# Two of batch 1's head pairs: x transposed by a DMA through the crossbar in place of TensorE, in a fused attention and GELU MLP kernel

## The chip, the cores and the metric

One core of one Trainium2 chip. The metric is the device time of one execution in microseconds. Engines: PE (TensorE; PEld its weight loads), DVE (VectorE), ACT (ScalarE), POOL (GpSimd) and SP (SyncE, which here only issues DMAs), and 16 DMA engines that carry the transfers of all queues.

## What is computed

The inputs are q, k, v of 8 batches x 8 heads x 576 tokens x 64, forget gates f of 8 x 8 x 576, and the weights w_in (512 x 2048) and w_out (2048 x 512), all float32.

```python
scores = (1 / sqrt(64)) * q @ k.T                     # per batch and head
cum    = cumsum(log(clip(f, 1e-4, 1)), axis=-1)
scores = where(causal, -1e9, scores + cum[:, None] - cum[None, :])
attn   = softmax(scores)                              # over the keys
x      = (attn @ v), heads side by side               # 4608 x 512
h      = x @ w_in
out    = (0.5 * h * (1 + erf(h / sqrt(2)))) @ w_out   # 4608 x 512
```

## The kernel before

Batches run one after the other. In each, the eight heads are taken as four pairs, since two heads of 64 fill 128 partitions.

**Attention of a pair.** `scores(b, i, t)` multiplies kT by qT into a tile of the score pool (two buffers of PSUM), four tiles t per pair; ACT takes the exponential (L313) and POOL zeroes the half above the diagonal (L315), except in batch 0 and pair 0 of batch 1, where PE adds the mask. `attend` multiplies the exponentials by the weighted v (L334); the decay is folded into v as a factor per key, which POOL multiplies in (`weigh_v`, L272). `normalize` divides by the row sums on DVE and writes x of the pair (L347, L348): 128 tokens x 5 blocks x 128 (two heads x 64), bfloat16.

**x to xT.** The MLP's first product needs x with the model dimension on the partitions. There are two ways in the program. `to_xT(b, i, ...)` has PE transpose five 128x128 blocks into a PSUM buffer (L367), and DVE or ACT copies that into `xT` (L370). `x_dma(b, i)` issues one DMA_TRANSPOSE from SBUF to SBUF on SP's queue (L373), straight into `xT`. Batches 0 and 1 use `to_xT` for all four pairs; batches 2 to 7 use `x_dma` for all four.

**MLP.** `gemm1` multiplies w_in by xT in 16 blocks of the hidden dimension, of four matmuls each (L389), and ACT takes the GELU (L409). The second product is interleaved with the next batch's attention (`gemm2_first` L529, `gemm2_second` L553, `gemm2_rows` L493, `take(fill, n)` issuing n of its steps). A batch has 576 = 512 + 64 tokens; the 64 left over are kept in `tails` (`x_tail`, POOL, L379) and multiplied last, for all batches together (L389 and L433 at the end).

**The order around the change.** The program fixes the order by hand; every engine takes its instructions in the order in which the program issues them, and an instruction waits for the semaphores of what it reads and of the buffer that it writes. In `second_attention` (batch 1) PE's order is: score tiles and attention of pairs 0 to 3, with `gemm1_hold` (six blocks of batch 0's GEMM1, kept in SBUF for a later GELU) and `gemm2_first` in between; then `gemm1_begin`, whose first matmuls read pairs 0 and 1 of xT, and the rest of batch 1's GEMM1. `gemm2_third` follows in batch 2's attention, beginning with `gemm2_second`: its first 8 steps write two banks of the PSUM pool "o", which DVE adds to `ot` (L561, then L513 through `sum_out`), its next 8 two banks of pool "m" in the same way; then `gemm2_rows` takes the two "o" banks again (L493).

**Transfers.** POOL's queue (q0) loads with a cast from float32 to bfloat16: q and k of the next batch (`load_qk_tokens`, L109), w_in and w_out (L171, L175), and v of batch 1 (L121). SP's queue (q1) carries v of later batches (L121), the transposes, and the stores (L517). From batch 2 on, q and k are transposed by DMA as well: `transpose_dma(2, 0, 4)` and `(2, 4, 8)` issue a tq and a tk transpose for four heads each (L239), on SP; tq waits for q, tk for k. DVE's `untangle` then puts them into qT and kT (L253), for pairs 0 to 3 of batch 2 at hidden blocks 5, 8, 11 and 14 of batch 1's GEMM1, ahead of the additions L561 and L513 in DVE's order. `behind(qk_of[2][1], H - 1)` is a POOL copy that reads the last of batch 2's k (L579), so that the last two w_out loads are issued after k has landed.

Of the kernel before, what the change touches and what calls it, by code (L numbers as in the profile page):

```python
# [53 lines left out]
def kernel(  # L54
# [10 lines left out]
    nc = tc.nc  # L65
# [25 lines left out]
    o_psum = ctx.enter_context(tc.tile_pool(name="o_psum", bufs=2, space=PSUM))  # L91
# [81 lines left out]
    def load_w_out(c):  # L173
        kt = slice(c * n_ff // 4, (c + 1) * n_ff // 4)
        nc.gpsimd.dma_start(w_out_sb[:, kt, :], w_out_r[:, kt, :])  # L175
# [27 lines left out]
    def transposes_first(b, i, which, pool, tag, late=False):  # L203

        src = qk_of[b][which]
        ps = pool.tile([P, JT, PT], BF16, tag=tag, name="ps_f")
        for j in range(JT):
            for h in range(2):
                nc.tensor.transpose(  # L209
                    ps[h * D : (h + 1) * D, j, :],  # L210
                    src[:, 2 * i + h, j * D : (j + 1) * D],
                    ident_bf[:PT, :PT],
                )

        dst = (qT, kT)[which][i].rearrange("d (p j) -> d p j", j=JT)
        src = ps.rearrange("d j p -> d p j")
        if late:
            return partial(nc.vector.tensor_copy, dst, src)
        if b or i:
            nc.vector.tensor_copy(dst, src)  # L220
        elif which:
            nc.vector.tensor_copy(dst[:, 0 : PT // 2], src[:, 0 : PT // 2])
            nc.scalar.copy(dst[:, PT // 2 :], src[:, PT // 2 :])
        else:
            nc.scalar.copy(dst, src)
# [3 lines left out]
    def transpose_dma(b, h0, h1):  # L229

        if b >= B:
            return
        if b not in tq_of:
            tq_of[b] = [
                tq_pool.tile([P, H, JT // 2, PT], BF16, tag="t" + n, name=f"t{n}{b}")
                for n in "qk"
            ]
        for src, dst in zip(qk_of[b], tq_of[b]):
            nc.sync.dma_start_transpose(  # L239
                dst[:, h0:h1].rearrange("d h j p -> d (h j) p"),  # L240
                src[:, h0:h1].rearrange("p h c -> p (h c)"),
            )
# [19 lines left out]
    def vw(b):  # L262
        if b not in vw_of:
            vw_of[b] = v_pool.tile([P, H, NBLK, D + 1], BF16, tag="vw", name=f"vw{b}")
        return vw_of[b]

    def weigh_v(b, i, eng=nc.gpsimd, n0=0, n1=NBLK):

        hs = slice(2 * i, 2 * i + 2)
        bh = b * H + 2 * i  # L270
        w = wT[:, n0:n1, bh : bh + 2].rearrange("p n h -> p h n")
        eng.tensor_tensor(  # L272
            vw(b)[:, hs, n0:n1, 0:D],
            v_sb[:, hs, n0:n1, :],
            w.unsqueeze(3).to_broadcast([P, 2, n1 - n0, D]),
            Alu.mult,
        )
        if b:
            eng.tensor_copy(vw(b)[:, hs, :, D], w)
# [47 lines left out]
    def attend(b, i, h, ms, pool=o_psum, tag="o"):  # L327
        if (b, i, h) not in o_of:
            o_of[b, i, h] = pool.tile([P, NBLK, D + 1], FP32, tag=tag, name="o")
        o = o_of[b, i, h]  # L330
        for m in ms:
            for n in range(m + 1):
                t, c = where(n, m)
                nc.tensor.matmul(  # L334
                    o[:, m, :],
                    e_of[b, i, t][:, h, c : c + P],
                    vw_of[b][:, 2 * i + h, n, :],
                    start=(n == 0),
                    stop=(n == m),
                )  # L340

    def normalize(b, i, h):
        if (b, i) not in x_of:
            x_of[b, i] = x_pool.tile([P, NBLK, 2, D], BF16, tag="x", name="x")
        o = o_of[b, i, h]
        r = x_pool.tile([P, NBLK], FP32, tag="r", name="r")
        nc.vector.reciprocal(r, o[:, :, D])  # L347
        nc.vector.tensor_tensor(  # L348
            x_of[b, i][:, :, h, :],
            o[:, :, 0:D],  # L350
            r.unsqueeze(2).to_broadcast([P, NBLK, D]),
            Alu.mult,
        )

    def xT(b):
        if b not in xT_of:
            xT_of[b] = xT_pool.tile([P, n_dm, XC], BF16, tag="xT", name="xT")
        return xT_of[b]

    def to_xT(b, i, copy, pool=m_psum, tag="m", ps=None):  # L360
        if ps is None:
            shape = [P, 2, 1024] if pool is s_psum else [P, XC]
            ps = pool.tile(shape, BF16, tag=tag, name="ps_x")
            if pool is s_psum:
                ps = ps[:, 0, 0:XC]
        for m in range(NBLK):
            nc.tensor.transpose(  # L367
                ps[:, m * P : (m + 1) * P], x_of[b, i][:, m, :, :], ident_bf
            )
        copy(xT(b)[:, i, :], ps)  # L370

    def x_dma(b, i):
        nc.sync.dma_start_transpose(  # L373
            xT(b)[:, i, :].rearrange("d (m p) -> d m p", p=P),
            x_of[b, i].rearrange("p m h d -> p (m h d)"),
        )
# [37 lines left out]
    def gemm1_hold(ffb, copy=nc.vector.tensor_copy):  # L414
        ps = gemm1(0, ffb, act=False)
        h_of[ffb] = h_pool.tile([P, TC], FP32, tag=f"h{ffb}", name=f"h{ffb}")
        copy(h_of[ffb], ps)
# [103 lines left out]
    def gemm2_first(c):  # L521

        pss = [
            m_psum.tile([P, d_model], FP32, tag="m", name="ps2") for _ in range(2)
        ]
        for kq in (0, 4):
            for ts in range(2):
                for kt in range(kq, kq + 4):
                    nc.tensor.matmul(  # L529
                        pss[ts],  # L530
                        g_of[c][kt][:, ts * P : (ts + 1) * P],
                        w_out_sb[:, kt, :],
                        start=(kt == 0),
                        stop=(kt == 7),
                    )
                    if kt == 7:
                        ot_of.append(
                            o_pool.tile([P, d_model], FP32, tag="ot", name="ot")
                        )
                        copy = nc.scalar.copy if ts else nc.vector.tensor_copy  # L540
                        copy(ot_of[ts], pss[ts])
                    yield
# [27 lines left out]
    def take(gen, n):  # L570
        for _ in range(n):
            if next(gen, "end") == "end":
                return


    def behind(t, h):

        g = x_pool.tile([P, 1], FP32, tag="gate", name="gate")
        nc.gpsimd.tensor_copy(g[:PT], t[:, h, 0:1])  # L579
# [166 lines left out]
    def second_attention():  # L746


        b, fill = 1, gemm2_first(0)

        def av(i, h):
            attend(b, i, h, (0, 1, 2, 3, 4))
            normalize(b, i, h)

        def transposes(i, pool, tag):
            for which in range(2):
                transposes_first(b, i, which, pool, tag)


        nc.scalar.activation(warm[0:1, 0:1], warm[0:1, 0:1], Act.Exp)  # L760
        def tiles(i, t):
            scores(b, i, t)
            scores(b, i, t + 1)

        def run(i):
            av(i, 0)
            av(i, 1)

        tiles(0, 0)
        transposes(1, o_psum, "o")  # L770
        gemm1_hold(10)
        gemm1_hold(11)
        tiles(0, 2)
        gemm1_hold(12, nc.scalar.copy)
        transposes(2, o_psum, "o")
        tiles(1, 0)
        gemm1_hold(13)
        run(0)
        tiles(1, 2)
        gemm1_hold(14, nc.scalar.copy)  # L780
        transposes(3, o_psum, "o")
        weigh_v(1, 2)
        tiles(2, 0)
        gemm1_hold(15)
        run(1)
        weigh_v(1, 3)
        tiles(2, 2)
        take(fill, 4)
        tiles(3, 0)
        transpose_dma(2, 0, 4)  # L790
        transpose_dma(2, 4, 8)
        to_xT(b, 0, nc.vector.tensor_copy, o_psum, "o")
        to_xT(b, 1, nc.vector.tensor_copy, o_psum, "o")
        take(fill, 4)
        tiles(3, 2)
        behind(qk_of[2][1], H - 1)
        load_w_out(2)
        load_w_out(3)
        run(2)
        take(fill, 4)  # L800
        av(3, 0)
        take(fill, 4)
        both = s_psum.tile([P, 2, 1024], BF16, tag="s", name="ps_x2")
        to_xT(b, 2, nc.scalar.copy, ps=both[:, 0, 0:XC])
        av(3, 1)
        gemm1_begin(1, both)
        x_tail(1)
        load_v(2)
# [71 lines left out]
```

## Time and profile before

| | |
|---|---|
| three runs | 334.89, 335.05, 335.53 us (median 335.05) |
| the profiled execution | 337.87 us, its span 335.9 us |
| busy: PE | 325.7 us (97%) |
| busy: ACT | 206.6 us (61%) |
| busy: DVE | 184.2 us (55%) |
| busy: POOL | 133.0 us (40%) |
| granted TensorE clock | 1.0 throughout |
| DMA | 44.16 MB, mean 131 GB/s |
| xT<-x, issued by SP | 24 transposes, median 2.7 us from issue to landing |
| tq<-q, tk<-k, issued by SP | 12 and 12 transposes, median 4.2 and 4.3 us |

"Busy" is the time in which an engine executes something; the span is the profiled stretch from the first to the last instruction. In lines of the profile, L367 is line 367 of the kernel, `xT<-x` means that xT is written from x, and a bracket gives the idle time before an instruction and what ended it. Times in views are microseconds from the start of the span. The DMA share of a stretch can exceed 100% where an engine has more than one packet under way.

### The profile page before, as it was taken

How to read it: one execution, taken by the hardware profiler on the slowest of the kernel's cores; microseconds unless marked ns; L12 is line 12 of the kernel's file. 1: busy time of each engine (PE TensorE's matmuls, PEld its weight loads, DVE VectorE, ACT ScalarE, POOL GpSimd, SP SyncE). 2: the span in 40 equal slices, each digit the busy share in tenths (PEclk: the TensorE clock that was granted, in tenths of full speed). 3: DMA queues.
4: the chain of work that ended last, by engine and by line, in shares of the span. 5: the costliest groups of instructions: out<-in, count | busy, mean ns of one | idle time of the engine just before them, and what ended most of it. 6: DMA issues, size and time to landing. Idle time of an engine off the chain costs nothing.

```text
span 335.9 us, 7819 instructions
## 1 busy us (share of the span) xinstructions
PE 325.7 (97%) x3161; PEld 170.7 (51%) x3161; DVE 184.2 (55%) x424; ACT 206.6 (61%) x298; POOL 133.0 (40%) x260
## 2 busy tenths in 40 slices
PE   7779999999999999999999999999999999999995
PEld 3564555445554456445644555446544654444443
DVE  5671666594358945894579547964696550020011
ACT  4957886983734787378827882788378846404600
POOL 8787874029437044723445344525441420000000
PEclk9999999999999999999999999999999999999999
DMA  8999998999998799599947995769800231011012
GB/s 117 188 187 219 194 189 116 158 181 158 207 205 175 120 204 185 102 140 149 212 128 108 170 195 157 112 119 192 195 13 2 87 72 49 0 72 54 0 45 81
DMA packets 97427, 44.16 MB, mean 131 GB/s; under 512 B 75728, under 2 KB 92368, under 8 KB 97392
## 3 DMA queue, kind: packets, MB, share of 16 engines
q1 hardware_dynamic: 79344, 27.55, 41.6%
q0 software_dynamic: 17648, 15.60, 30.5%
q8 instruction: 24, 0.39, 0.5%
q10 hardware_dynamic: 400, 0.52, 0.4%
q14 instruction: 11, 0.09, 0.1%
HBM read 36.85 MB, written 9.44 MB: 138 GB/s over the span
## 4 chain that ended last, share of the span: by engine, by line
PE 90%; DMA 4%; POOL 2%; issue 1%; DVE 1%; ACT 0%; POOLq 0%; ACTq 0%
PE ps L389 36%; PE ps L493 26%; PE o L334 9%; PE ps L433 8%; PE s L303 7%; DMA v_sb<-in_v_dram 2%; DMA xT<-x 1%; PE ps L553 1%; PE ps_x L367 1%; PE ps L529 1%; PE ps_f L209 1%; POOL k L109 1%; POOL q L109 1%; DVE vw L272 0%; ACT e L313 0%
## 5 line engine op out<-in xcount | busy, mean ns | idle before, releaser
L409 ACT ACTIVATE g<-ps 128x512 bf16<-128x512 f32 x138 | 78.5, 601 | 79.8 <-PE ps L389 79.3
L313 ACT ACTIVATE e<-s 128x896 bf16<-128x896 f32 (+2 forms) x128 | 100.2, 835 | 23.8 <-PE s L303 18.7
L389 PE MATMUL ps<-xT,w_in_sb 128*128 128x512 bf16 x512 | 113.6, 379 | 0.1
L493 PE MATMUL ps<-w_out_sb,g 64*128 64x512 bf16 (+1 forms) x711 | 108.0, 377 | 0.0
L389 PEld LDWEIGHTS <-w_in_sb 128*128 128x128 bf16 x576 | 55.5, 98 | 67.4 <-issue 3.1
L315 POOL TENSOR_SCALAR_AFFINE_SELECT e<-e 128x256 bf16<-128x256 bf16 (+1 forms) x135 | 49.1, 383 | 90.1 <-ACT e L313 89.9
L493 PEld LDWEIGHTS <-g 64*128 64x128 bf16 (+1 forms) x711 | 39.4, 95 | 34.7 <-issue 4.2
L272 POOL TENSOR_TENSOR vw<-v_sb,wT 128x640 bf16<-128x640 f32 x30 | 38.7, 1290 | 26.1 <-DMA v_sb<-in_v_dram 15.3
L303 PE MATMUL s<-qT,kT 64*128 64x320 bf16 (+4 forms) x384 | 42.9, 276 | 1.5 <-ACT e L313 0.7
L253 DVE COPY kT<-tk 64x288 bf16<-64x288 bf16 x96 | 42.8, 446 | 1.6
L253 DVE COPY qT<-tq 64x288 bf16<-64x288 bf16 x96 | 40.0, 417 | 5.1 <-DMA tq<-q 3.7
L334 PEld LDWEIGHTS <-e 128*128 128x128 bf16 x960 | 34.7, 98 | 9.6 <-POOL e L315 2.9
L501 DVE COPY ot<-ps 128x512 f32<-128x512 f32 x20 | 13.8, 692 | 46.5 <-PE ps L493 46.5
L334 PE MATMUL o<-vw,e 128*128 128x65 bf16 x960 | 37.1, 194 | 1.3 <-DVE vw L272 1.3
L348 DVE TENSOR_TENSOR x<-o,r 128x320 bf16<-128x320 f32 x64 | 31.5, 492 | 3.1 <-DVE r L347 0.7
L442 DVE COPY ot<-ps 128x512 f32<-128x512 f32 (+2 forms) x9 | 5.7, 632 | 49.6 <-PE ps L433 49.6
L303 PEld LDWEIGHTS <-kT 64*128 64x128 bf16 x384 | 19.2, 94 | 21.5 <-issue 4.8
L433 PE MATMUL ps<-w_out_sb,g 128*128 128x512 bf16 (+2 forms) x144 | 28.0, 355 | 0.0
L433 PEld LDWEIGHTS <-g 128*128 128x128 bf16 x144 | 13.5, 98 | 14.5
L347 DVE RECIPROCAL r<-o 128x5 f32<-128x5 f32 x64 | 12.1, 188 | 11.3 <-PE o L334 11.3
L513 DVE TENSOR_TENSOR ot<-ot,ps 128x512 f32<-128x512 f32 x22 | 15.1, 685 | 1.1
L389 PE MATMUL ps<-tails,w_in_sb 128*128 128x512 bf16 x64 | 14.3, 378 | 0.0
(69 smaller groups left out, 153.6 us busy)
## 6 DMA issues: line engine op xcount, KB each, us to landing
out_dram<-ot SPq DMA_DIRECT2D x32, 256.0 KB, 2.4
v_sb<-in_v_dram SPq DMA_DIRECT2D x24, 256.0 KB, 4.8
q<-in_q_dram POOLq DMA_DIRECT2D x6, 576.0 KB, 6.3
k<-in_k_dram POOLq DMA_DIRECT2D x6, 576.0 KB, 8.4
w_in_sb<-in_moe_w_in_dram POOLq DMA_DIRECT2D x4, 512.0 KB, 8.0
w_out_sb<-in_moe_w_out_dram POOLq DMA_DIRECT2D x4, 512.0 KB, 9.2
v_sb<-in_v_dram POOLq DMA_DIRECT2D x13, 128.0 KB, 7.1
v_sb<-in_v_dram SPq DMA_DIRECT2D x9, 128.0 KB, 4.7
```

The lines of the kernel that those rows point to most:

```text
L253: nc.vector.tensor_copy(rows[:, odd], src[odd * D : (odd + 1) * D, 2 * i + h].rearrange("d j p -> d p j"),)
L272: eng.tensor_tensor(vw(b)[:, hs, n0:n1, 0:D], v_sb[:, hs, n0:n1, :], w.unsqueeze(3).to_broadcast([P, 2, n1 - n0, D]), Alu.mult,)
L303: nc.tensor.matmul(to, *ab, start=half < 0, stop=half == 1 or not masked)
L313: nc.scalar.activation(et[:, :, z:c], st[:, :, z:c], Act.Exp, scale=scale)
L315: nc.gpsimd.affine_select(out=et[:, :, c0 + z : c0 + P], in_=et[:, :, c0 + z : c0 + P], compare_op=Alu.is_ge, fill=0.0, base=z, pattern=[[ ...
L334: nc.tensor.matmul(o[:, m, :], e_of[b, i, t][:, h, c : c + P], vw_of[b][:, 2 * i + h, n, :], start=(n == 0), stop=(n == m),)
L348: nc.vector.tensor_tensor(x_of[b, i][:, :, h, :], o[:, :, 0:D], r.unsqueeze(2).to_broadcast([P, NBLK, D]), Alu.mult,)
L389: nc.tensor.matmul(ps, w_in_sb[:, kt, ffb * P : (ffb + 1) * P], src[:, kt, 0:TC], start=(kt == 0), stop=(kt == n_dm - 1),)
L409: nc.scalar.activation(g_of[c][ffb], ps, Act.Gelu)
L433: nc.tensor.matmul(pss[ts][:, c0:c1], g_of[c][kt][:, ts * P : (ts + 1) * P], w_out_sb[:, kt, c0:c1], start=(kt == 0), stop=(kt == n_ff - 1),)
L493: nc.tensor.matmul(banks[r], g_of[c][kt][rows, ts * P : (ts + 1) * P], w_out_sb[rows, kt, :], start=kt == (steps.index("r") if r else 0), ...
L513: nc.vector.tensor_tensor(ot, ot, bank, Alu.add)
```

## The change

In `second_attention`, batch 1's x of pairs 0 and 1 is no longer transposed by PE (`to_xT`, ten matmuls at L367 into two buffers of the pool "o", two DVE copies at L370). Instead `x_dma` is issued for each of the two pairs, right after the attention of that pair: pair 0 after `run(0)`, pair 1 after `run(1)`. On SP's queue both stand ahead of batch 2's transposes of q and k and of batch 2's v loads; before, nothing stood there between the first v loads of batch 0 and those transposes. Pairs 2 and 3 stay with PE. The first matmuls of batch 1's GEMM1 wait for the two transfers instead of the copies.

```diff
@@ second_attention
         gemm1_hold(13)
         run(0)
+        x_dma(b, 0)
         tiles(1, 2)
         gemm1_hold(14, nc.scalar.copy)
         transposes(3, o_psum, "o")
...
         gemm1_hold(15)
         run(1)
+        x_dma(b, 1)
         weigh_v(1, 3)
         tiles(2, 2)
         take(fill, 4)
         tiles(3, 0)
         transpose_dma(2, 0, 4)
         transpose_dma(2, 4, 8)
-        to_xT(b, 0, nc.vector.tensor_copy, o_psum, "o")
-        to_xT(b, 1, nc.vector.tensor_copy, o_psum, "o")
         take(fill, 4)
         tiles(3, 2)
```

## The prediction

> **What bounds the kernel now.** I read the page first, then the chain of waits around the change, then the transfer queues stretch by stretch, and last the timelines of SP, VectorE and TensorE behind the change. The page gives the frame.
>
> ```profile
> PE 325.7 (97%) x3161; PEld 170.7 (51%) x3161; DVE 184.2 (55%) x424; ACT 206.6 (61%) x298; POOL 133.0 (40%) x260
> ...
> DMA  8999998999998799599947995769800231011012
> ```
>
> TensorE (PE) is busy for 97% of the span, so a microsecond taken from it, or a wait put into it, goes straight to the end. But the 16 DMA engines are full too, in nearly every slice up to 120 us, and the change sits at 44 to 56 us. The chain shows what the edit takes away:
>
> ```profile
> 48.18 0.72 issue
> 48.90 0.71 ACT e L313
> 49.61 0.04 issue
> 49.65 0.34 PE s L303 x4
> 49.99 0.66 PE ps_x L367 x10
> 50.65 0.86 PE ps L529 x4
> 51.52 0.43 PE s L303 x4
> ```
>
> The ten transposes of pairs 0 and 1 are on the path with 0.66 us. Ahead of them PE waits for exponentials of ACT, which stays. From here on PE has no gap over 0.12 us until 332 us.
>
> **What is removed.** Ten matmuls: -0.66 us. Part of it comes back at once: the scores of pair 3, tiles 2 and 3, then start at 50.86, and tile 3 writes the score buffer that ACT frees with the last of four exponentials (start 48.09, 3.05 us together, so 51.14). PE is there at 50.86 + 0.21 = 51.07 and goes on near 51.18: +0.11. Everything up to the dense GEMM1 at 57.33 depends on PE, or on ACT and POOL work that PE releases, so it moves as one: **-0.55**. The two VectorE copies (0.89 us, L370) lie between idle times of 1.69 and 1.26 us: nothing. The two PSUM buffers that they held are not waited for now: nothing.
>
> **What is added.** Two crossbar transposes on SP's queue. Their x is ready at 43.81 + 0.49 = 44.30 and at 48.23 + 0.49 = 48.72. SP meanwhile only waits:
>
> ```profile
> 50.35 1.36 SPq L239 DMA_TRANSPOSE tq<-q  x1
> 53.24 1.31 SPq L239 DMA_TRANSPOSE tk<-k  x1
> 54.59 2.13 SPq L239 DMA_TRANSPOSE tq<-q  x1
> 56.76 6.73 SPq L239 DMA_TRANSPOSE tk<-k  x1
> ```
>
> The first row started when batch 2's q had landed, the second when its k had (issued at 40.08, 13.1 us to landing: 53.2). Issuing an xT transpose takes SP 1.2 to 2.4 us (24 rows of L373), so both are out by about 50 and SP's time costs nothing. By the program's waits an SP transfer also waits for the one eight before it; two more shift these pairs, but the earlier ones (the new transposes among them, for the v loads from 63.6 on) have long landed. GEMM1 now waits for the two landings: its first matmuls come at 55.90 - 0.55 = 55.35. The 24 xT transposes land in 2.4 to 4.8 us; the longest, which began beside q and k loads, puts the second at 53.5. Margin 1.8 us: nothing, unless it is held up (a rival below).
>
> The cost is what the transposes take from the loads. Three stretches of the transfer view price that; the first is q and k loads alone, the second w_out loads (q0) beside transposes (q1), the third q1 alone:
>
> ```profile
> q0 software_dynamic: 1056, 0.80, 129.5%
> ```
> ```profile
> q0 software_dynamic: 616, 0.61, 91.2%
> q1 hardware_dynamic: 613, 0.16, 31.5%
> ```
> ```profile
> q1 hardware_dynamic: 3457, 0.87, 134.7%
> ```
>
> All three are 4 us long (45 to 49, 61 to 65, 68 to 72). Packets of the two queues alternate one for one, and the engines have no room left. One x is 128 x 640 x 2 bytes = 163,840, at 256 bytes 640 packets; two are 1,280. Alone they take 1280 / (3457 / 4 us) = 1.5 us of all engines. In the mix, w_out packets run at 154 a us, against some 190 in the stretches where they are alone: 613 transpose packets cost 4 - 616/190 = 0.76 us, 1,280 cost 1.6. The low end is the first x alone, 0.75, if k is nearly through when the second comes (from 50 on). k's last engine still has 2.5 us of work then, so I take **1.5** for the delay of k, with 0.75 and 1.6 as ends.
>
> The Trainium skill speaks against the change: "VectorE: DVE Perf Modes", "Rules for kernel authors", advises TensorE for a 128x128 transpose where PSUM will do, and its section "The three transpose paths" gives 390 ns on TensorE against 1309 ns on the crossbar. The row here is 66 ns each on TensorE; by the page's 390 the ten would free 3.9 us and the sum would start at -3.9, an estimate that the row contradicts. "Advanced Engine Details and Errata", "X-Bar Transpose (TRN2)", expects 350 to 400 GB/s, which would make the two 0.8 to 0.95 us, an estimate, and the sum below about +0.4.
>
> **Where k's delay arrives.** tk's issue waits for k: +1.5. The last two w_out loads stand on POOL behind a copy that reads k (L579). That copy ran at 53.85, 0.6 after k, because of POOL's own selects, which now end earlier; so w_out moves only by 1.5 - 0.6 = 0.9. w_out and the second half of tq and tk share the engines until 67, so their end moves by 0.9 to 1.5; I take 1.2. That half is waited for by VectorE:
>
> ```profile
> 67.07 1.34 DVE L253 COPY qT<-tq 64x288 bf16<-64x288 bf16 x4 [3.68 <-DMA tq<-q]
> ...
> 71.13 1.34 DVE L253 COPY kT<-tk 64x288 bf16<-64x288 bf16 x4
> 72.51 0.69 DVE L561 TENSOR_TENSOR ot<-ot,ps 128x512 f32<-128x512 f32 x1
> 73.23 0.69 DVE L513 TENSOR_TENSOR ot<-ot,ps 128x512 f32<-128x512 f32 x1
> ```
> ```profile
> 74.23 1.89 PE L493 MATMUL ps<-w_out_sb,g 64*128 64x512 bf16 x16
> ```
>
> This is the reading that decides. VectorE idles 3.68 us for tq, untangles two pairs without a pause (5.4 us), and only then adds up and frees the two "o" banks of PSUM (L561, L513, end 73.92), which the row block at 74.23 takes on PE. Its slack is 74.23 - 73.92 - 0.04 = 0.27 us. So a landing that is late by d moves PE's path by d - 0.27, and never below the -0.55 that PE itself gains. Even with d = 0 half the gain is gone. With d = 1.2: the copies start at 68.27, the banks are free at 75.12, PE goes on at 75.16 in place of 74.23: **+0.93**.
>
> Others behind the same transfers have room. v lands about 1.2 later, so POOL's weighing moves from 73.69 to 74.9 and its selects end at 81.0 in place of 79.76, for an attention block that PE now reaches at 81.73 + 0.93: covered. w_out is needed from 70.4, its last part about a us later, and landed at 66.9: covered. The first half of tk landed at 58.3 and is needed at 70.2. After 76 us nothing else that I see turns the delay into more, nor is there PE idle time in which to win it back.
>
> **The sum.** The profiled execution took 337.87 us, 335.9 of it span and 1.97 around it; the three runs have a median of 335.05, 2.82 lower. I carry the difference over: 335.05 + 0.93 = 335.98, about 336.0.
>
> **Rivals.** *A pause of the crossbar.* Sometimes all transfers halt when a transpose sets in. The stretch from 56 to 61 us has one, from 59.2 to 60.8:
>
> ```profile
> GB/s 6 33 98 74 33 16 0 8 41 82 51 49 49 25 197 178 174 188 190 197 172 174 193 143 137 66 25 12 10 10 0 8 0 0 8 16 8 12 86 193
> ```
>
> The packet records have 12 such places, of 0.5 to 2.1 us (mean 1.2), for 48 transposes: one in four, so 0.44 for at least one in two more. One adds about 1.2, making +2.1 (337.2); two +3.4. Against it: these pauses may as well replace ones that are there.
>
> *The delay is absorbed, so not slower.* The mechanism is that very pause at 59 us. It lies between k's landing and tq's second half. If the later order of transfers avoids it, 1.6 us come back, d falls to -0.4, and PE keeps its gain: -0.55 + 0.0, 334.5 (with d = 0: -0.27, 334.8). It decides from d under 0.27 on. For it: pauses come and go with small shifts. Against it: the pause sits where w_out and tq meet, and they still meet.
>
> *The second x lands after GEMM1 needs it.* tq's second half took 12.5 us to land; a second x with that would come at 61.2, 5.9 late. But that one queued behind a whole tk; the second x queues behind one small x. Late by 0.5 to 2, on top of the landing delay in part: about +1.5 to +2.5 (337).
>
> **How the numbers follow.** Forecast (delay of 0.6 to 1.9 without a new pause, +0.3 to +1.6, so 335.4 to 336.7): 0.42. A new pause: 0.25. Absorbed: 0.26. Second x late: 0.07. A difference of 0.2%, 0.67 us, is about what a measurement of this kernel tells from none. Of the forecast 0.28 lies above +0.67 and 0.14 below; with the pause (0.25) and the late x (0.07), slower is 0.60. Absorbed ends at -0.55, inside 0.2% but next to its edge; I put 0.10 of it beyond and 0.16 inside: faster 0.10, and same 0.14 + 0.16 = 0.30. The range runs from 334.4 (full gain, and a little) to 337.6, in the middle of the one-pause case; two pauses are left out.
>
> **What would show it.** Right: no L367 for pairs 0 and 1, the scores of pair 3 about 0.55 earlier; batch 2's q and k landing 1 to 2 us later; the first untangle copy that waits for tq's second half at about 68.3; a PE gap of about 1.5 us ahead of the row block at L493 after the two L553 blocks, filled by L513 in the chain. Wrong: the untangle copies still near 67 (then PE keeps 0.3 to 0.5), a wait of L389 on xT near 55, or a gap that arises at another place.

## The result, and the profile after

The changed kernel took 336.19 us (median of 22 runs, 335.57 to 340.85) against 335.43 us (22 runs, 334.12 to 338.57) of the kernel before: +0.76 us by the medians. The ratio is 1.0038, with a 95% interval of 1.002 to 1.0057, so +0.7 to +1.9 us. The profiled execution took 339.98 us, span 337.8; it is one of four among the 22 runs above 338.5, so its waits are probably larger than the usual ones. The same caution holds for the experiments: the profiled executions of r1_again, r4_pair0 and b12_after_skip are the slowest of their twelve runs, and that of b9_before is the fastest of its twelve. What a profile shows below is shown for that execution; only the medians and intervals speak for the usual one.

The chain of waits of the changed kernel, in order of time (start, length, what), has two places that the chain before does not have:

```profile
46.24 10.03 DMA xT<-x
56.28 0.04 issue
56.32 0.81 PE ps L389 x3
...
74.32 0.70 DVE ot L561
75.02 0.02 issue
75.04 0.70 DVE ot L513
75.74 0.04 issue
75.78 3.66 PE ps L493 x31
```

First, GEMM1 (L389) waits for the second x, which landed 10.03 us after it was issued. Second, the row block (L493) waits for the two PSUM banks that DVE adds up. PE's timeline has the lengths, in brackets:

```profile
56.32 0.81 PE L389 MATMUL ps<-xT,w_in_sb 128*128 128x512 bf16 x3 [3.10 <-DMA xT<-x]
```
```profile
75.06 0.37 PE L493 MATMUL ps<-w_out_sb,g 64*128 64x512 bf16 x1 [0.60 <-DVE ot L561]
75.78 1.47 PE L493 MATMUL ps<-w_out_sb,g 64*128 64x512 bf16 x12 [0.35 <-DVE ot L513]
```

SP's timeline answers to the one shown of before:

```profile
41.83 5.77 SPq L373 DMA_TRANSPOSE xT<-x  x2
51.05 1.33 SPq L239 DMA_TRANSPOSE tq<-q  x1
56.12 1.28 SPq L239 DMA_TRANSPOSE tk<-k  x1
57.45 1.60 SPq L239 DMA_TRANSPOSE tq<-q  x1
59.09 6.35 SPq L239 DMA_TRANSPOSE tk<-k  x1
```

PE reached this stretch 2.5 us earlier than in the profile before (pair 3's first score tile at 46.55, not 49.05), because the start of that one profiled execution was slow. Yet tk is issued 2.9 us later. So the profile before is a poor measure of the transfers; a second one, b9_before below (span 332.5), is the one to compare with. Its DVE and PE timelines:

```profile
63.79 1.34 DVE L253 COPY qT<-tq 64x288 bf16<-64x288 bf16 x4 [3.46 <-DMA tq<-q]
...
70.02 0.69 DVE L513 TENSOR_TENSOR ot<-ot,ps 128x512 f32<-128x512 f32 x1
```
```profile
71.17 1.89 PE L493 MATMUL ps<-w_out_sb,g 64*128 64x512 bf16 x16
```

The last L513 ends at 70.71, so the banks' slack is 71.17 - 70.71 - 0.04 = 0.42 us.

### The profile page after: what moved, and what is told of

Same layout as the page of the kernel before. It is cut to its first block, busy times and chain, and to the rows that moved or that the text cites. A ratio compares the mean times of both kernels' runs of the same rounds, so it can differ in the third digit from the quotient of the medians.

```text
span 337.8 us, 7802 instructions
## 1 busy us (share of the span) xinstructions
PE 326.1 (97%) x3151; PEld 171.1 (51%) x3151; DVE 183.5 (54%) x422; ACT 206.5 (61%) x298; POOL 133.7 (40%) x260
## 4 chain that ended last, share of the span: by engine, by line
PE 88%; DMA 6%; POOL 2%; DVE 2%; issue 1%; POOLq 0%; DVEq 0%
PE ps L389 37%; PE ps L493 26%; PE o L334 8%; PE ps L433 8%; PE s L303 7%; DMA xT<-x 4%; DMA v_sb<-in_v_dram 2%; PE ps L553 1%; PE ps_f L209 1%; POOL q L109 1%; POOL k L109 1%; PE ps_x L367 1%; DVE x L348 0%; DVE qT L220 0%; DVE vw L272 0%
## 5 line engine op out<-in xcount | busy, mean ns | idle before, releaser
L389 PE MATMUL ps<-xT,w_in_sb 128*128 128x512 bf16 x512 | 113.7, 379 | 3.3 <-DMA xT<-x 3.3
L493 PE MATMUL ps<-w_out_sb,g 64*128 64x512 bf16 (+1 forms) x711 | 108.5, 377 | 0.9 <-DVE ot L561 0.6
L389 PEld LDWEIGHTS <-w_in_sb 128*128 128x128 bf16 x576 | 55.5, 98 | 70.9 <-issue 6.6
L493 PEld LDWEIGHTS <-g 64*128 64x128 bf16 (+1 forms) x711 | 40.3, 95 | 35.7 <-issue 5.7
L303 PE MATMUL s<-qT,kT 64*128 64x320 bf16 (+4 forms) x384 | 43.6, 276 | 1.7 <-ACT e L313 1.1
L253 DVE COPY kT<-tk 64x288 bf16<-64x288 bf16 x96 | 43.8, 457 | 1.6
L501 DVE COPY ot<-ps 128x512 f32<-128x512 f32 x20 | 13.8, 692 | 46.8 <-PE ps L493 46.8
L334 PEld LDWEIGHTS <-e 128*128 128x128 bf16 x960 | 34.5, 98 | 8.1 <-POOL e L315 2.5
L334 PE MATMUL o<-vw,e 128*128 128x65 bf16 x960 | 37.0, 194 | 0.1
L513 DVE TENSOR_TENSOR ot<-ot,ps 128x512 f32<-128x512 f32 x22 | 15.1, 685 | 1.1
L389 PE MATMUL ps<-tails,w_in_sb 128*128 128x512 bf16 x64 | 14.3, 378 | 0.0
```

The lines of the kernel that those rows point to most:

```text
L253: nc.vector.tensor_copy(rows[:, odd], src[odd * D : (odd + 1) * D, 2 * i + h].rearrange("d j p -> d p j"),)
L303: nc.tensor.matmul(to, *ab, start=half < 0, stop=half == 1 or not masked)
L334: nc.tensor.matmul(o[:, m, :], e_of[b, i, t][:, h, c : c + P], vw_of[b][:, 2 * i + h, n, :], start=(n == 0), stop=(n == m),)
L389: nc.tensor.matmul(ps, w_in_sb[:, kt, ffb * P : (ffb + 1) * P], src[:, kt, 0:TC], start=(kt == 0), stop=(kt == n_dm - 1),)
L493: nc.tensor.matmul(banks[r], g_of[c][kt][rows, ts * P : (ts + 1) * P], w_out_sb[rows, kt, :], start=kt == (steps.index("r") if r else 0), ...
L513: nc.vector.tensor_tensor(ot, ot, bank, Alu.add)
```

## The experiments

Two theories. **A, the landing:** GEMM1 waits for the second x. **B, the banks:** the transposes delay batch 2's q and k, hence the second half of tq, hence DVE's untangling and the additions that free the banks. Kernels of one table share the runs of the kernel before; its median stands in the last column.

### First four: again, only the transfers, neither, one pair

r1_again is the changed kernel as it is.

> The changed kernel once more, beside the kernel before. Its profile has two waits that the kernel before has not: PE's GEMM1 (L389) waits 3.10 us for the landing of the second xT, and the row block L493 waits for the two PSUM banks that VectorE frees late (L561, L513). Theory A, the landing: the wait of L389 is the bulk of the loss and comes back here with 1 to 3 us. Theory B, the banks: the loss is the late untangling that ends in L513; then the L389 wait is an accident of one execution and is under 0.5 us here, and PE's gap before L493 is 0.6 to 1.5 us. Time: +0.8 to +1.6 us on either.

r2_dma_extra adds the transfers and takes nothing away (its lines after the new helper count 8 higher: L397, L501, L521 and L569 are L389, L493, L513 and L561):

```diff
+    scratch = consts.tile([P, 2, XC], BF16)
+    def x_spare(b, i):
+        nc.sync.dma_start_transpose(
+            scratch[:, i, :].rearrange("d (m p) -> d m p", p=P),
+            x_of[b, i].rearrange("p m h d -> p (m h d)"),
+        )
...
         run(0)
+        x_spare(b, 0)
...
         run(1)
+        x_spare(b, 1)
```

> TensorE keeps its ten transposes as before, and the two crossbar transposes are issued as well, at the changed kernel's places, into a scratch tile that nobody reads. So the transfers are added and nobody waits for their landing. Theory A, the landing: nothing waits, so the time is that of before, within 0.3 us. Theory B, the banks: q, k and then tq's second half are still late by d = 1.2 to 2 us, the wait before L493 is d - 0.27, and the time is +0.9 to +1.7 us.

r3_neither takes the matmuls away and adds no transfer:

```diff
-        to_xT(b, 0, nc.vector.tensor_copy, o_psum, "o")
-        to_xT(b, 1, nc.vector.tensor_copy, o_psum, "o")
+        nc.vector.memset(xT(b)[:, 0:2, :], 0.0)
```

> Pairs 0 and 1 of batch 1's x are not transposed at all: neither the ten matmuls and two copies nor the two DMAs; one VectorE memset puts zeros into that half of xT (its output lacks these pairs). The most that the removal can bring. Theory A: nothing but PE's path counts, -0.55 us. Theory B: tq's second half still lands near where it did, so the banks hold PE back by 0.28 us before L493 and the gain is -0.27 us.

r4_pair0 changes one pair:

```diff
         run(0)
+        x_dma(b, 0)
...
-        to_xT(b, 0, nc.vector.tensor_copy, o_psum, "o")
         to_xT(b, 1, nc.vector.tensor_copy, o_psum, "o")
```

> Only pair 0 goes through the crossbar (issued after run(0)); pair 1 is transposed by TensorE as before. The first x has some 4 us more until GEMM1 needs it. Theory A, the landing: no wait at L389, PE gains half of its transposes, -0.3 us. Theory B, the banks: half of the transfer load is left, k is late by about 0.8 and tq's second half by 0.5 to 1.0, so the wait before L493 stays with 0.5 to 1.0 us and the time is +0.2 to +0.7 us.

| kernel | median us | ratio to before (95%) | median before |
|---|---|---|---|
| r1_again | 336.55 | 1.0023 (1.0005 to 1.0041) | 335.67 |
| r2_dma_extra | 336.64 | 1.0041 (1.0018 to 1.0063) | 335.67 |
| r3_neither | 335.14 | 0.9984 (0.9966 to 1.0001) | 335.67 |
| r4_pair0 | 335.73 | 1.0027 (0.9997 to 1.0057) | 335.67 |

r1's profile has the wait of L389 again, 3.40 us, and hardly one at L493: PE is by then so late (a stretch at half clock followed the wait, see the last section) that the banks are free. The two waits are in series, and the first hides the second.

r2 has nobody who waits for a landing, and the transfers alone make it slower by about what the change does. In its DVE and PE timelines the loss stands at the banks:

```profile
66.58 1.35 DVE L253 COPY qT<-tq 64x288 bf16<-64x288 bf16 x4 [1.60 <-DMA tq<-q]
...
72.74 0.69 DVE L521 TENSOR_TENSOR ot<-ot,ps 128x512 f32<-128x512 f32 x1
```
```profile
72.76 0.37 PE L501 MATMUL ps<-w_out_sb,g 64*128 64x512 bf16 x1 [1.24 <-DVE ot L569]
73.48 1.89 PE L501 MATMUL ps<-w_out_sb,g 64*128 64x512 bf16 x15 [0.35 <-DVE ot L521]
```

tq's half is untangled d = 66.58 - 63.79 = 2.79 us later than in b9_before, and the row block runs on at 73.48 in place of 71.17, 2.31 later; d less the slack of 0.42 is 2.37. The same holds for the changed kernel: d = 68.87 - 63.79 = 5.08, less 0.42 is 4.66, and the row block is 75.78 - 71.17 = 4.61 later. In r4, d = 66.93 - 63.79 = 3.14, less 0.42 is 2.72; measured 73.84 - 71.17 = 2.67. So B's arithmetic is right in the profiles of three kernels. In r2 these 2.31 us are most of the 3.0 us by which its profile's span (335.6) exceeds that of b9_before. And r2's time, for which A expected that of before, refutes A as the sole cause.

r3 shows what the removal is worth: from pair 3's first score tile to GEMM1's first matmul PE takes 52.32 - 46.03 = 6.29 us, against 52.84 - 45.99 = 6.85 in b9_before: 0.56 us, and -0.53 by the medians. Its interval just includes no change.

r4 has the bank wait without a wait at L389, as B expected, but longer (1.50 and 0.35 us, where 0.5 to 1.0 was expected); its time is split (eight runs from 334.9 to 336.0, four from 337.9 to 339.3), so nothing is concluded from its median.

### Second four: the fourth pair untangled after the additions

The same edit on four kernels: r2 (e5_extra_late), the changed one (e6_after_late), r4 (e7_pair0_late) and the one before (e8_before_late).

```diff
-                if late == 0:
+                if late == 0 and (b, at) != (1, 3):
                     untangle(b + 1, at)
...
                 take(fill, counts[i][t])
+                if b == 2 and (i, t) == (0, 1):
+                    untangle(2, 3)
```

> As r2_dma_extra (TensorE transposes kept, both crossbar transposes issued into a scratch tile), but batch 2's fourth pair is untangled after the additions that free the banks (in batch 2's attention, after score tile 1 of pair 0) and not ahead of them: 2.7 us less VectorE work in front of L561 and L513. The transfers stay as late as they were. Theory B (the loss goes through the banks): the wait before L493, 1.59 us in r2's profile, falls to 0 and so does the time's difference, 0 within 0.3 us. If the transfers cost at another place as well, +0.5 us or more stays.

> The changed kernel with the fourth pair untangled late in the same way. The waits of L389 for the second xT (3.10 and 3.40 us in two profiles) and for the banks (0.95 and none) are in series on PE. Theory A+B: the bank wait goes, the L389 wait stays at about 3 us; the time is 0 to 0.5 us under the changed kernel, so +0.3 to +1.0 us against before. Theory B alone: -0.5 us against before.

> As r4_pair0 (pair 0 by crossbar, pair 1 by TensorE) with the fourth pair untangled late. r4's profile has no wait of L389 and 1.85 us before L493. Both theories: neither wait is left and TensorE's gain of five transposes shows, -0.3 us (0 to -0.6). If this comes out over 0, the transfers cost PE something that neither wait holds.

> The kernel before with the fourth pair untangled late: the control. Its profile has no wait at the banks, so 0 within 0.3 us; if it is faster by more, the banks held PE in the kernel before too, in executions without a profile, and e5 to e7 have to be read against this one.

| kernel | median us | ratio to before (95%) | median before |
|---|---|---|---|
| e5_extra_late | 340.72 | 1.013 (1.0084 to 1.0176) | 335.29 |
| e6_after_late | 341.18 | 1.0153 (1.0118 to 1.0189) | 335.29 |
| e7_pair0_late | 341.46 | none given | 335.29 |
| e8_before_late | 340.59 | 1.0134 (1.0097 to 1.0171) | 335.29 |

A miss: the control e8 loses 5.3 us as well, so the times answer nothing about A and B. The moved copies now run beside POOL's weighing and selects, and stretch. The groups of e8's DVE, first from 64 to 69 us where POOL is idle, then from 72.4 to 81 (busy us, mean ns of one; the four qT copies there took 632 ns on average):

```profile
L253 DVE COPY kT<-tk 64x288 bf16<-64x288 bf16 x4 | 1.3, 326 | 0.1
```
```profile
L253 DVE COPY kT<-tk 64x288 bf16<-64x288 bf16 x4 | 5.8, 1457 | 0.1
```

The eight copies end at 80.9, the next bank's additions come after them, and the attention block waits 2.90 us (PE o L334 <- DVE ot L501 in e8's waits). One thing is usable: in e5's profile tq's half is untangled at 66.61, as late as in r2, L561 waits 0.52 us for PE and not the other way round, and PE has no gap before the row block. With less DVE work ahead of the additions the bank wait is gone, though the transfers are as late. In e6's profile GEMM1 waits for the second x too, 1.15 us, less than the 3 that were expected.

### Last four: the fourth pair not untangled at all

This takes the same work away without putting it beside POOL. Pair 3's scores of batch 2 then read what batch 1 left. b10_before_skip, b11_extra_skip and b12_after_skip have the first hunk of the diff above on the kernel before, r2 and the changed kernel; b9_before is the kernel before unchanged.

> The kernel before once more, for a second profile beside the one on record, whose PE ran some 2.5 us later against the transfers than in all profiles of this study. Theory A+B: PE is free of waits between 47 and 332 us, batch 2's k lands at 51 to 52 and tq's second half between 62.5 and 65, so the banks are free 0 to 1 us ahead of PE. Time 0 within 0.3 us.

> The kernel before without the untangling of batch 2's fourth pair (that pair's scores then read what batch 1 left in qT and kT), so that VectorE has 2.7 us less work in front of the additions that free the banks, and none is moved beside POOL's work. Control: the banks do not hold PE in the kernel before, so 0 within 0.3 us.

> TensorE's transposes kept, both crossbar transposes issued into a scratch tile as in r2_dma_extra, and the fourth pair of batch 2 not untangled (its scores read what batch 1 left). The transfers are as late as in r2. Theory B (all that they cost goes through the banks): PE has no wait before the row block, and the time is that of before within 0.3 us, where r2 was +1.0. If the transfers cost elsewhere too: +0.5 or more.

> The changed kernel without the untangling of batch 2's fourth pair (its scores read what batch 1 left). The bank wait is taken away, the wait for the second xT stays. Theory A+B: L389 waits 1 to 3.5 us in the profile and the time stays at +0.5 to +1.0 us. Theory B alone (the L389 wait is only in series with the bank wait and not the cause): -0.5 us.

| kernel | median us | ratio to before (95%) | median before |
|---|---|---|---|
| b9_before | 335.19 | 0.998 (0.9954 to 1.0005) | 335.38 |
| b10_before_skip | 335.46 | 0.9999 (0.9972 to 1.0027) | 335.38 |
| b11_extra_skip | 336.98 | 1.0049 (1.0017 to 1.0081) | 335.38 |
| b12_after_skip | 335.62 | 1.0011 (0.998 to 1.0043) | 335.38 |

b9 and b10: as expected, the banks do not hold PE in the kernel before.

b12: the profile has no bank wait, and L389 waits 2.66 us for the second x:

```profile
45.80 9.59 DMA xT<-x
55.39 0.04 issue
55.44 0.81 PE ps L389 x3
```

So in this execution the landing wait is there without the bank wait. The time decides less: the median is at +0.24 us, under the +0.5 to +1.0 expected, and the interval, -0.7 to +1.4 us, holds the -0.5 of B alone as well. That the median lies under the two of the changed kernel (+0.76 and +0.88) looks as if the banks were half a microsecond or more of it, but the intervals overlap.

b11 misses, and it speaks against B as the whole account of r2's time. Its profile is as B wants it (DVE waits for PE ahead of the additions, and not the reverse),

```profile
69.49 0.69 DVE L569 TENSOR_TENSOR ot<-ot,ps 128x512 f32<-128x512 f32 x1 [1.44 <-PE ps L561]
```

yet the kernel is no faster than r2. In its profile batch 2's GEMM1 starts at 98.81, level with b9_before's 98.61, and the last batch's part is 1.03 us late; of that 0.83 arises in later batches, 0.57 of it in one batch that takes 35.39 us in place of 34.82, around a wait of 0.26 us for an xT transpose near 171 us (r2's profile has such a wait in the same batch, 0.30 us; b9_before's has none). The profiled execution lies at 335.93, in the lower part of its runs. What makes the others slower is not shown.

## Why the prediction was right, and where it was not

**The sum.** 336.0 was predicted, with +0.93; 336.19 was measured, +0.76 by the medians and +1.27 by the ratio. Sign, size and range hold. That the size fits is in part luck: the delay of k was off by 1.1 us and more in the profiles of r2 and the changed kernel, a wait that the sum put at nothing was there with 1.15 to 3.40 us, and no run shows what the loss is made of in the usual execution. Of the signs named ahead, the late untangling and the gap ahead of L493 came, and so did one of those for being wrong, the wait of L389 on xT near 55.

**TensorE's gain, -0.55.** Right: 0.56 in r3's profile, and 0.55 in b12's (52.40 - 46.10 = 6.30, from the score tile to GEMM1).

**SP's time and the DVE copies at nothing.** Right: tq is issued at 51.05 in the changed kernel, just as q lands (issued at 38.56, 12.5 us).

**"A landing late by d moves PE's path by d less the slack".** Right within 0.06 us in the profiles of three kernels. This was the step said to decide. In r2's profile it is most of the loss; b11, as slow as r2 without the wait, leaves open how much of the medians it is. The slack was read as 0.27 from a profile with a slow start; in b9_before it is 0.42.

**The delay of k, 1.5, and d, 1.2.** Mis-sized for the profiled executions. The transfer view gives k's time from issue to landing between 37 and 57 us; b9_before, r2 and the changed kernel:

```profile
k<-in_k_dram POOLq DMA_DIRECT2D x1, 576.0 KB, 12.5
```
```profile
k<-in_k_dram POOLq DMA_DIRECT2D x1, 576.0 KB, 15.1
```
```profile
k<-in_k_dram POOLq DMA_DIRECT2D x1, 576.0 KB, 16.8
```

That is +2.6 and +4.3, and d was 2.79 and 5.08. The price per packet is not enough for it: r4, with one x and so half the packets, has k at 15.1 as well, while b11, with both, has it at 14.0. What was left to a rival is there each time: a pause. In the changed kernel's transfers from 47 to 48.1 us both queues nearly stop,

```profile
GB/s 168 47 130 65 0 56 65 37 19 65 0 19 28 0 37 0 9 28 0 9 0 0 28 0 9 28 0 9 0 28 0 9 28 0 0 74 233 130 158 195
```

after the first x's packets begin among q's and k's (packets held for up to 1.31 us), and again from 54.7 to 56.1, just before k lands. The 1.5 us of the prediction and these two pauses, 1.1 and 1.4, add up to 4.0 of the 4.3 us (an estimate). All nine profiles with a transpose of x beside these loads show the first pause, for 0.4 to 1.2 us at under half the packet rate before it; b9_before, r3 and b10 have none there. I had put 0.44 on one in two transposes. The usual execution must lose less than the profiled one: the measured +0.76 to +1.27 asks for d of 1.2 to 1.7 if the formula holds there and nothing waits at L389, which no run shows.

**The landing of the second x, "margin 1.8 us: nothing".** This step failed. It rested on the xT rows of batches 2 to 7, 2.4 to 4.8 us, of which the longest was to stand for a transfer beside loads. Here the two took (the changed kernel, L373, 40 to 60 us):

```profile
DMA to landing us min/median/max: 9.5/9.7/10.0
```

In all profiles with x transposed at this place it was 7.0 to 11.2. From 38 to 45 us the changed kernel's transfer view has 1,224 packets of q0 and none of q1, though the first x was issued at 41.83: it got its first packet at 45.81. In all nine profiles that took 3.94 to 4.00 us from the issue, whether the last w_out load ahead of it landed 0.8 us before that packet (b11) or 1.2 us after it (r1), so that load does not explain it. In the kernel before, the first transpose, tq, had its first packet 1.28 us after its issue. What makes the 4 us is open. Then came the pause, then the one-for-one share with q and k. The row that was nearest in kind (tq's second half beside w_out, 12.5 us) was put aside as an exception; it was nearer than the xT rows. The rival had 0.07; the wait that it names stands in all four profiles of kernels whose GEMM1 reads both transposed x (3.10, 3.40, 1.15 and 2.66 us), though its time, about 337, is that of slower executions than the usual one. It should have had far more weight.

**Absorbed.** Not seen: in no profile with the transposes did tq's half come as early as in b9_before.

**What stays open.** How the loss divides in the usual execution between the two waits and whatever slows b11 (its +1.6 us), what holds the first x for 4 us, and what starts a pause. A kernel that beats both was not found: the most that the removal can bring is the -0.53 us of r3, at the edge of what the runs can tell, and with both pairs the transposes took more than that each time.

## What to carry to other kernels

A transfer that replaces compute is better priced by the queue that it joins than by its own duration elsewhere (here 7.0 to 11.2 us, not 2.4 to 4.8): look up the landing time of the nearest transfer in the same stretch, beside the same loads, and take the long one. Then follow what the displaced loads feed, through each engine's order, to the first place where the bound engine waits; the lateness less the slack there gives the loss in that execution. How late the usual execution is, one profile does not tell. Two waits in series hide one another, so an experiment that takes one away needs the other's length beside it, and a control with the edit alone.

## What the runs showed that I had not expected

**The clock after a wait.** In some executions the granted TensorE clock falls to half for 3.41 us (6.83 in e6 and e7) after PE has waited. The windows of r4_pair0 from 74.1 to 77.6 us and of b9_before in the same stretch; the column after the engines' busy times is the clock:

```profile
core 0: us, PE busy (x) PEld busy (x) DVE busy (x) ACT busy (x) POOL busy (x), PEclk, DMA share, GB/s
74.10:77.60 3.50, 3.50 (x21) 1.65 (x18) 0.97 (x2) 0.17 (x1) 3.50 (x6) 0.51 0.40 150
```
```profile
74.10:77.60 3.50, 3.50 (x40) 1.77 (x38) 1.38 (x2) 1.41 (x2) 3.50 (x8) 1.00 0.83 106
```

PE issues about half as many matmuls, so a wait of 1.85 us costs about 1.7 us more. It came after waits of 1.50 + 0.35 (r4), 2.66 (b12), 3.40 (r1) and 2.90 us (e8), and not after 3.10 in the changed kernel or 1.24 + 0.35 in r2. The length of the wait alone does not decide. In each profile the changes of the clock lie on one grid of 3.41 us, and the idle time of PE inside a single cell of it sorts the cases: cells with 1.85 us (r4), 2.37 (e6), 2.41 (e7), 2.59 (b12) and 2.98 (r1) were followed by half clock at once, one with 1.95 (e8) a cell later, and those with 1.35 and 1.75 (the changed kernel, whose wait lies across an edge) and 1.59 (r2) were not. The Trainium skill, "TensorE: Matmul & The Clock Gate", section "What's actually happening", gives a free-running window of 3413 ns and half rate after an idle one; the length and the free-running grid agree, but here less than a whole window of idle time was enough, 1.85 us in r4 and 2.59 in b12. Of the 16 runs above 338.5 us of the changed kernel, r1, r2, r4, b11 and b12, ten have a mean clock of 0.993 to 0.995, which fits one such stretch.

**VectorE copies beside GpSimd.** 326 ns for a kT copy alone became 1457 on average, and 3.58 us at the longest, in e8. The skill's "SBUF — State Buffer", section "Who interferes with whom", says that copies in a two-port mode and GpSimd exclude each other for a whole instruction; the longest copy is more than twice POOL's longest instruction there (1.37 us), so it lost the port more than once if that is the cause, which no run tests.
